# Stores of g on ScalarE's queue, and single-bank sums for the last products

## The chip, the cores and the metric

The kernel runs on one core of one Trainium2 chip. The metric is the device time of one execution in microseconds (us): here the median of three runs. Beside it stands one profiled execution, whose trace the text reads. A core has five engines with a queue of their own: TensorE (PE, matrix products into PSUM), VectorE (DVE), ScalarE (ACT), GpSimd (POOL) and SyncE (SP, which here only issues DMA transfers). Each works its queue off in order; semaphores tie them together.

## The reference

A retention layer (attention with a decaying state) and behind it a two-layer feed-forward block:

```python
for t in range(S):
    state = gamma[None, :, None, None] * state + np.einsum('bhd,bhe->bhde', k[:, :, t], v[:, :, t])
    y[:, :, t] = scale * np.einsum('bhd,bhde->bhe', q[:, :, t], state)
...
h = x @ w_in
relu6 = np.clip(h + 3.0, 0.0, 6.0)
g = h * relu6 / 6.0
return (g @ w_out).astype(np.float32)
```

q, k and v have shape (4, 8, 768, 64), so x has 3072 tokens of 512 values; w_in is 512 x 2048 and w_out 2048 x 512. The weights arrive as 64-bit floats.

## The kernel before

The tokens are cut into six tiles of 512 (`u` = 0 to 5, `UT` = 512), the 2048 inner columns into 16 blocks of 128 (`jj`).

**First phase, lines 473 to 499.** For every pair (`u`, `jj`) `mm1` (line 459) computes one tile of h: 12 products on TensorE into one PSUM bank (three buffers, `ps_h`), then a relu on ScalarE (line 468), then a multiplication with a bound of 6 on VectorE (line 469), which leaves g in SBUF (three buffers, `hpool`), then a store of g to memory (line 470), 256 KB, issued by SP. The 12 products are 4 blocks of the inner dimension times 3: each operand is split by `split` (line 139, ScalarE and VectorE at lines 140 and 141) into a rounded part and a rest, and three of the four products of parts are summed.

Between these tiles TensorE does the attention in bursts (`burst`, line 260, in the first half of the tokens, `chunk_burst`, line 355, in the second); a state in PSUM (`uz`) is copied out by ScalarE (lines 323 and 353) before TensorE adds the next piece. The rows of k, q and v that a burst needs are loaded by SP (`load`, line 218), and some of them are multiplied on GpSimd (lines 231, 235, 245).

In the same stretch the weights are built. `fetch` (line 109) has SP load a block of 64-bit words into a tile `st` (two buffers); `to_f32` (line 114) makes 32-bit floats of it with five operations on VectorE (lines 122 to 136) and one on ScalarE (line 126); then they are split. The first four blocks of w_in are fetched with the attention's first rows; the further ones by the loop over `steps`, line 486, the fifth between the first and the second tile of h. Blocks of w_out follow at the places that `WHEN` lists.

**Second phase, lines 502 to 615.** Tiles of g are read back from memory into `gv`, two blocks of a pair and two token tiles at a time, summed or subtracted (a scheme with seven products of blocks in the place of eight), split into `gc`, and multiplied with w2 (line 587): three super-blocks `sb`, in each four groups of sums (`GROUPS`), in each four steps `c`. The sums `acc` of groups 0 and 2 stand on the right side of PSUM, those of 1 and 3 on the left; a sum is one tile of two banks, one for each half `h` of its output rows. At the end of a group VectorE or ScalarE reads the sums (lines 534 and 537), and SP stores the output (line 541). The last group of the last super-block is read and stored in halves (`parts`).

**What sets the order.** TensorE's order is that of the program (`manual_schedule`). On the other engines the framework orders the instructions of a queue by its own estimate, with hints such as `high_priority` and `issue_after`; once ordered, the queue is fixed. It also finds the semaphores that an instruction must wait for, by tile. Of the two first-phase queues that the change touches, SP's holds all loads and all stores in one line.

Of the kernel before, what the change touches and what calls it, by code (L numbers as in the profile page):

```python
# [19 lines left out]
P = 128  # L20
# [8 lines left out]
def retention_ffn(ctx: ExitStack, tc: tile.TileContext, qkv, w_in, w_out, dvs, dqs, dkc, dqc, dmc, out, B, H, S, D):  # L29
# [429 lines left out]
    def mm1(u, jj):  # L459
        h = ps_h.tile([P, UT], F32, tag="h", name=nm("h"))  # L460
        for k in range(NK):
            t, o = w1_block(jj, k)
            for n, (a, b) in enumerate(((0, 0), (0, 1), (1, 0))):
                nc.tensor.matmul(  # L464
                    h, t[:, o, a], xs[u][b][:, k], start=k + n == 0, stop=(k, n) == (NK - 1, 2), skip_group_check=True
                )
        g = hpool.tile([P, UT], F32, tag="g", name=nm("g"))
        nc.scalar.activation(out=g, in_=h, func=AF.Relu, bias=three)  # L468
        ins = nc.vector.scalar_tensor_tensor(out=g, in0=g, scalar=6.0, in1=h, op0=ALU.min, op1=ALU.mult)  # L469
        nc.sync.dma_start(out=gd[jj // 2][:, jj % 2, u * UT : (u + 1) * UT], in_=g)  # L470
        return ins.ins

    order = ExitStack()
# [8 lines left out]
    for n, (u, jj) in enumerate(steps):  # L482
        if (u, jj) == (NU - 1, 0):
            att.close()
            late = ctx.enter_context(tc.tile_pool(name="late", bufs=1, side="right", reuse_waits="tile"))
        while n_w1 < min(NF, jj + 4):
            build_w1(n_w1)
            n_w1 += 1
        if jj in WHEN.get(u, ()):
            build_w2(n_w2)  # L490
            n_w2 += 1
        end = mm1(u, jj)
        if n < UR:
            advance(UR + 2 + n)
        elif u == 1:
            advance(2 * UR + 2 + int((jj + 1) / NF * UR + 0.5))
        elif 1 < u < NU - 1:
            advance(UR * (u + 1) + 2 + int((jj + 1) / NF * UR + 0.5))
    ph1.close()

# [3 lines left out]
        for n in ("gv0", "gv1", "gc2", "v", "p", "gc0", "gc1", "q")  # L504
    }
    ps_o = [
        ctx.enter_context(tc.tile_pool(name=f"ps_o{i}", bufs=1, space=PSUM, reuse_waits="tile", side=side))
        for i, side in enumerate(("right", "left"))
# [29 lines left out]

    def store(sb, t, m, src, h):
        o = out[m * HM : (m + 1) * HM, (2 * sb + t) * UT : (2 * sb + t + 1) * UT].rearrange("(h p) n -> p h n", p=P)  # L540
        nc.sync.dma_start(out=o[:, h], in_=src[:, h])

    for sb in range(NT // TB):
        for g, ids in enumerate(GROUPS):
            acc = {i: ps_o[g % 2].tile([P, 2, UT], F32, tag=f"o{n}", name=nm("o")) for n, i in enumerate(ids)}
            for c in range(NFP // CP):
# [35 lines left out]
                for i, gc in zip(ids, ops):  # L582
                    for h in range(2):
                        for jj in range(CP):
                            j = c * CP + jj
                            for n, (x, y) in enumerate(((0, 0), (0, 1), (1, 0))):
                                nc.tensor.matmul(  # L587
                                    acc[i][:, h],
                                    w2c[j][:, RIGHT[i], x, h],
# [4 lines left out]
                                )  # L594
            whole = slice(0, 2)
            if g == 0:
# [6 lines left out]
            elif g == 2:  # L603
                acc6(kept["u"], acc[7], kept["u"])
                dve_add(kept["p"], kept["u"], kept["p"])
                dve_add(kept["q"], kept["u"], kept["q"])
                store(sb, 1, 0, kept["p"], whole)
                store(sb, 1, 1, kept["q"], whole)
            else:
                parts = (whole,) if sb < NT // TB - 1 else (slice(0, 1), slice(1, 2))  # L610
                for k, i, m in (("s", 2, 0), ("v", 3, 1)):
                    for h in parts:
                        acc6(kept[k][:, h], acc[i][:, h], kept[k][:, h])
                        store(sb, 0, m, kept[k], h)
    order.close()
# [97 lines left out]
```

## Time and profile before

| what | value |
|---|---|
| three runs | 590.0, 590.01, 592.35 us |
| median | 590.01 us |
| the profiled execution | 590.15 us |
| its span, first to last instruction | 588.4 us |
| mean granted TensorE clock | 0.992 |
| moved to and from memory | 117.05 MB, mean 199 GB/s |
| transfers of g to memory | 96 of 256 KB, all issued by SP |

The span is the part of the profiled execution in which instructions run; 1.75 us lie around it. A line such as `L469 DVE` names the line of the kernel and the engine; where a row has a bracket, it is the idle time of that engine just before the instruction, and the instruction that ended it. `PEclk` or the clock column is the share of TensorE's full clock that was granted. A transfer has an issue (busy time in its issuer's queue) and a time to landing that comes after.

### The profile page before, as it was taken

How to read it: one execution, taken by the hardware profiler on the slowest of the kernel's cores; microseconds unless marked ns; L12 is line 12 of the kernel's file. 1: busy time of each engine (PE TensorE's matmuls, PEld its weight loads, DVE VectorE, ACT ScalarE, POOL GpSimd, SP SyncE). 2: the span in 40 equal slices, each digit the busy share in tenths (PEclk: the TensorE clock that was granted, in tenths of full speed). 3: DMA queues.
4: the chain of work that ended last, by engine and by line, in shares of the span. 5: the costliest groups of instructions: out<-in, count | busy, mean ns of one | idle time of the engine just before them, and what ended most of it. 6: DMA issues, size and time to landing. Idle time of an engine off the chain costs nothing.

```text
span 588.4 us, 11368 instructions
## 1 busy us (share of the span) xinstructions
PE 573.7 (98%) x4604; PEld 471.3 (80%) x4604; DVE 416.6 (71%) x588; ACT 249.1 (42%) x393; POOL 35.2 (6%) x39
## 2 busy tenths in 40 slices
PE   8888999999999999999999999999999999999996
PEld 7766788777888888888888888888888888888885
DVE  4879999999533498333225989769587698866871
ACT  5773445443423344332324555444335343344430
POOL 1001000101221121121000000000000000000000
PEclk9988999999999999999999999999999999999999
DMA  8966677665965467555243457564844747635611
GB/s 321 391 234 208 218 254 233 233 216 187 300 231 174 160 225 250 189 182 174 106 135 115 162 194 253 176 218 143 277 152 144 243 143 262 211 114 181 205 72 71
DMA packets 58884, 117.05 MB, mean 199 GB/s; under 512 B 5968, under 2 KB 6352, under 8 KB 58832
## 3 DMA queue, kind: packets, MB, share of 16 engines
q1 hardware_dynamic: 58688, 116.31, 58.7%
q8 instruction: 36, 0.59, 0.4%
q14 instruction: 16, 0.13, 0.1%
q10 hardware_dynamic: 144, 0.02, 0.0%
HBM read 84.85 MB, written 31.46 MB: 198 GB/s over the span
## 4 chain that ended last, share of the span: by engine, by line
PE 78%; DVE 14%; DMA 3%; issue 3%; ACT 1%; SPq 1%; DVEq 0%; ACTq 0%
PE o L587 39%; PE h L464 33%; DVE g L469 2%; DMA st<-in_w_in 2%; PE uz L349 2%; DVE w L141 2%; DVE wb L128 2%; PE sc L349 1%; DVE am L327 1%; DVE we L131 1%; DVE ww L134 1%; PE y L349 1%; DVE we L122 1%; DMA early<-in_qkv 1%; DVE wb L123 1%
## 5 line engine op out<-in xcount | busy, mean ns | idle before, releaser
L464 PE MATMUL h<-x,w 128*128 128x512 f32 x1152 | 271.1, 394 | 2.8 <-DVE x L141 1.2
L464 PEld LDWEIGHTS h<-x,w 128*128 128x128 f32 x1152 | 214.9, 189 | 51.4 <-DVE g L469 3.1
L587 PE MATMUL o<-gc,w 128*128 128x512 f32 x1008 | 231.5, 392 | 0.0
L587 PEld LDWEIGHTS o<-gc,w 128*128 128x128 f32 x1008 | 189.2, 188 | 42.1
L469 DVE SCALAR_TENSOR_TENSOR g<-g,h 128x512 f32<-128x512 f32 x96 | 65.3, 683 | 84.7 <-ACT g L468 84.7
L468 ACT ACTIVATE g<-h,three 128x512 f32<-128x512 f32 x96 | 65.2, 683 | 101.1 <-PE h L464 98.3
L140 ACT ACTIVATE gc<-gv 128x1024 fp32r<-128x1024 f32 x48 | 50.8, 1060 | 65.8 <-PE o L587 55.1
L141 DVE TENSOR_TENSOR gc<-gv,gc 128x1024 fp32r<-128x1024 f32 x48 | 58.6, 1221 | 22.8 <-ACT gc L140 22.7
L140 ACT ACTIVATE gc<-spare 128x1024 fp32r<-128x1024 f32 x36 | 38.2, 1061 | 48.9 <-PE o L587 37.5
L141 DVE TENSOR_TENSOR gc<-spare,gc 128x1024 fp32r<-128x1024 f32 x36 | 43.9, 1220 | 8.6 <-ACT gc L140 8.5
L140 ACT ACTIVATE w<-ww 128x384 fp32r<-128x384 f32 (+2 forms) x34 | 18.7, 555 | 49.0 <-DVE ww L134 46.6
L126 ACT ACTIVATE we<-we,ebias 128x512 int32<-128x512 int32 x32 | 22.9, 717 | 12.2 <-DVE we L122 12.2
L134 DVE SCALAR_TENSOR_TENSOR ww<-wb,we 128x512 f32<-128x512 f32 x32 | 24.5, 765 | 0.6
L235 POOL TENSOR_TENSOR qs<-qt,dq 128x512 f32<-128x512 f32 x12 | 16.7, 1388 | 95.9 <-PE y L349 59.9
L128 DVE SCALAR_TENSOR_TENSOR wb<-st,wb 128x512 f32<-128x512 uint32 x32 | 21.9, 685 | 0.2
L141 DVE TENSOR_TENSOR w<-ww,w 128x384 fp32r<-128x384 f32 (+2 forms) x34 | 19.9, 590 | 3.1 <-ACT w L140 3.1
L131 DVE SCALAR_TENSOR_TENSOR we<-st,we 128x512 int32<-128x512 int32 x32 | 21.9, 683 | 0.0
L96 DVE TENSOR_TENSOR spare<-gv 128x1024 f32<-128x1024 f32 x12 | 14.7, 1222 | 8.0 <-DMA gv<-gd 8.0
L122 DVE TENSOR_SCALAR we<-st 128x512 int32<-128x512 int32 x32 | 14.3, 446 | 8.3 <-DMA st<-in_w_in 8.1
L93 DVE TENSOR_TENSOR spare<-spare,gv 128x1024 f32<-128x1024 f32 x12 | 14.6, 1220 | 5.3 <-DMA gv<-gd 5.3
L93 DVE TENSOR_TENSOR gv<-gv 128x1024 f32<-128x1024 f32 x12 | 14.7, 1223 | 4.6 <-DMA gv<-gd 4.5
L241 ACT ACTIVATE early<-early,cst_sb 128x64 f32<-128x64 f32 x64 | 16.4, 335 | 3.6 <-DMA early<-in_qkv 3.6
(73 smaller groups left out, 395.8 us busy)
## 6 DMA issues: line engine op xcount, KB each, us to landing
gd<-g SPq DMA_DIRECT2D x96, 256.0 KB, 2.7
gv<-gd SPq DMA_DIRECT2D x48, 512.0 KB, 4.9
gv<-gd SPq DMA_DIRECT2D x48, 256.0 KB, 3.1
st<-in_w_in SPq DMA_DIRECT2D x16, 512.0 KB, 4.0
st<-in_w_out SPq DMA_DIRECT2D x16, 512.0 KB, 3.9
early<-in_qkv SPq DMA_DIRECT2D x28, 256.0 KB, 6.0
kt<-in_qkv SPq DMA_DIRECT2D x16, 256.0 KB, 3.8
qt<-in_qkv SPq DMA_DIRECT2D x16, 256.0 KB, 4.2
```

The costliest lines, as they stand in the source:

```text
L93: return nc.vector.tensor_tensor(out=out_, in0=a, in1=b, op=ALU.subtract)
L126: nc.scalar.activation(out=e, in_=e, func=AF.Relu, scale=8.0, bias=ebias)
L128: nc.vector.scalar_tensor_tensor(out=y, in0=lo.bitcast(U32), scalar=2.0**-32, in1=b, op0=ALU.mult, op1=ALU.add)
L131: nc.vector.scalar_tensor_tensor(out=e, in0=hi, scalar=-2147483648, in1=e, op0=ALU.bitwise_and, op1=ALU.bitwise_or)
L134: nc.vector.scalar_tensor_tensor(out=w, in0=y, scalar=2.0**-20, in1=e.bitcast(F32), op0=ALU.mult, op1=ALU.mult)
L140: nc.scalar.activation(out=hi, in_=src, func=AF.Copy)
L141: nc.vector.tensor_tensor(out=lo, in0=src, in1=hi, op=ALU.subtract)
L349: nc.tensor.matmul(out_, lhs, rhs, start=start, stop=True, skip_group_check=True)
L464: nc.tensor.matmul(h, t[:, o, a], xs[u][b][:, k], start=k + n == 0, stop=(k, n) == (NK - 1, 2), skip_group_check=True)
L468: nc.scalar.activation(out=g, in_=h, func=AF.Relu, bias=three)
L469: ins = nc.vector.scalar_tensor_tensor(out=g, in0=g, scalar=6.0, in1=h, op0=ALU.min, op1=ALU.mult)
L587: nc.tensor.matmul(acc[i][:, h], w2c[j][:, RIGHT[i], x, h], gc[:, y, jj], start=j == 0 and n == 0, stop=j == NFP - 1 and n == 2, skip_grou ...
```

## The change

Two parts. First, the store of a tile of g is no longer issued by SP at its place in the program. It is put on a list, and issued by ScalarE behind the relu of the next tile (`to_memory(relu.ins)`); the last one is issued behind the last multiplication (`to_memory(end)`). Second, in the last group of the last super-block each half of a sum is a PSUM tile of its own, of one bank; to make room for them the two pools of sums are closed first. The four halves are read and stored one by one, and the last half is read and stored in two pieces of 256 columns (`BLK`), the second piece stored by ScalarE.

```diff
--- before.py
+++ after.py
@@ -465,10 +465,20 @@
                     h, t[:, o, a], xs[u][b][:, k], start=k + n == 0, stop=(k, n) == (NK - 1, 2), skip_group_check=True
                 )
         g = hpool.tile([P, UT], F32, tag="g", name=nm("g"))
-        nc.scalar.activation(out=g, in_=h, func=AF.Relu, bias=three)
+        relu = nc.scalar.activation(out=g, in_=h, func=AF.Relu, bias=three)
         ins = nc.vector.scalar_tensor_tensor(out=g, in0=g, scalar=6.0, in1=h, op0=ALU.min, op1=ALU.mult)
-        nc.sync.dma_start(out=gd[jj // 2][:, jj % 2, u * UT : (u + 1) * UT], in_=g)
+        to_memory(relu.ins)
+        waiting.append((gd[jj // 2][:, jj % 2, u * UT : (u + 1) * UT], g))
         return ins.ins
+
+    waiting = []
+
+    def to_memory(after):
+
+        for out_, g in waiting[:1]:
+            with tc.issue_after(after):
+                nc.scalar.dma_start(out=out_, in_=g)
+        del waiting[:1]
 
     order = ExitStack()
     order.enter_context(tc.manual_schedule(engines={mybir.EngineType.PE}))
@@ -496,6 +506,7 @@
             advance(2 * UR + 2 + int((jj + 1) / NF * UR + 0.5))
         elif 1 < u < NU - 1:
             advance(UR * (u + 1) + 2 + int((jj + 1) / NF * UR + 0.5))
+    to_memory(end)
     ph1.close()
 
 
@@ -503,8 +514,9 @@
         n: ctx.enter_context(tc.tile_pool(name=f"left_{n}", bufs=1, reuse_waits="tile"))
         for n in ("gv0", "gv1", "gc2", "v", "p", "gc0", "gc1", "q")
     }
+    ends = ctx.enter_context(ExitStack())
     ps_o = [
-        ctx.enter_context(tc.tile_pool(name=f"ps_o{i}", bufs=1, space=PSUM, reuse_waits="tile", side=side))
+        ends.enter_context(tc.tile_pool(name=f"ps_o{i}", bufs=1, space=PSUM, reuse_waits="tile", side=side))
         for i, side in enumerate(("right", "left"))
     ]
     CP = 2
@@ -536,13 +548,19 @@
     def acc6(out_, ps, other):
         nc.vector.scalar_tensor_tensor(out=out_, in0=ps, scalar=SIXTH, in1=other, op0=ALU.mult, op1=ALU.add)
 
-    def store(sb, t, m, src, h):
+    def store(sb, t, m, src, h=slice(0, 2), to=slice(0, UT), eng=nc.sync):
         o = out[m * HM : (m + 1) * HM, (2 * sb + t) * UT : (2 * sb + t + 1) * UT].rearrange("(h p) n -> p h n", p=P)
-        nc.sync.dma_start(out=o[:, h], in_=src[:, h])
+        eng.dma_start(out=o[:, h, to], in_=src[:, h, to])
 
     for sb in range(NT // TB):
         for g, ids in enumerate(GROUPS):
-            acc = {i: ps_o[g % 2].tile([P, 2, UT], F32, tag=f"o{n}", name=nm("o")) for n, i in enumerate(ids)}
+            last = sb == NT // TB - 1 and g == len(GROUPS) - 1
+            if last:
+                ends.close()
+                ps_e = ctx.enter_context(tc.tile_pool(name="ps_e", bufs=1, space=PSUM, reuse_waits="tile", side="left"))
+            acc = {i: ps_o[g % 2].tile([P, 2, UT], F32, tag=f"o{n}", name=nm("o")) for n, i in enumerate(ids)} if not last else {
+                i: [ps_e.tile([P, UT], F32, tag=f"e{i}{h}", name=nm("o")) for h in range(2)] for i in ids
+            }
             for c in range(NFP // CP):
                 with ExitStack() as first:
                     if sb == 0 and g == 0 and c == 0:
@@ -585,14 +603,13 @@
                             j = c * CP + jj
                             for n, (x, y) in enumerate(((0, 0), (0, 1), (1, 0))):
                                 nc.tensor.matmul(
-                                    acc[i][:, h],
+                                    acc[i][h] if last else acc[i][:, h],
                                     w2c[j][:, RIGHT[i], x, h],
                                     gc[:, y, jj],
                                     start=j == 0 and n == 0,
                                     stop=j == NFP - 1 and n == 2,
                                     skip_group_check=True,
                                 )
-            whole = slice(0, 2)
             if g == 0:
                 scaled(kept["p"], acc[4], -SIXTH)
                 scaled(kept["q"], acc[5])
@@ -604,14 +621,19 @@
                 acc6(kept["u"], acc[7], kept["u"])
                 dve_add(kept["p"], kept["u"], kept["p"])
                 dve_add(kept["q"], kept["u"], kept["q"])
-                store(sb, 1, 0, kept["p"], whole)
-                store(sb, 1, 1, kept["q"], whole)
+                store(sb, 1, 0, kept["p"])
+                store(sb, 1, 1, kept["q"])
             else:
-                parts = (whole,) if sb < NT // TB - 1 else (slice(0, 1), slice(1, 2))
                 for k, i, m in (("s", 2, 0), ("v", 3, 1)):
-                    for h in parts:
-                        acc6(kept[k][:, h], acc[i][:, h], kept[k][:, h])
-                        store(sb, 0, m, kept[k], h)
+                    if not last:
+                        acc6(kept[k], acc[i], kept[k])
+                        store(sb, 0, m, kept[k])
+                    else:
+                        for h in range(2):
+                            for n in range(2 if (i, h) == (3, 1) else 1):
+                                to = slice(n * BLK, (n + 1) * BLK) if (i, h) == (3, 1) else slice(0, UT)
+                                acc6(kept[k][:, h, to], acc[i][h][:, to], kept[k][:, h, to])
+                                store(sb, 0, m, kept[k], h, to, nc.scalar if n else nc.sync)
     order.close()
```

## The prediction

> **What bounds the kernel now.** I read the busy times of the page first, then the busy times by stage, then the chain of work that ended last, and only then the queue that the change empties.
>
> ```profile
> PE 573.7 (98%) x4604; PEld 471.3 (80%) x4604; DVE 416.6 (71%) x588; ACT 249.1 (42%) x393; POOL 35.2 (6%) x39
> ```
>
> TensorE is busy 98% of the 588.4 us. A share over the whole span hides who leads in a stage, so here are three stages of 30 us (columns: stage, length, then busy time and count of PE, PEld, DVE, ACT, POOL, then granted clock, DMA share, GB/s).
>
> ```profile
> 30.00:60.00 30.00, 26.61 (x298) 21.23 (x299) 25.65 (x42) 15.79 (x44) 2.09 (x2) 0.89 0.64 214
> 60.00:90.00 30.00, 29.83 (x239) 24.21 (x239) 29.49 (x53) 14.92 (x27) 1.05 (x1) 1.00 0.72 236
> 90.00:120.00 30.00, 30.00 (x200) 24.45 (x198) 29.76 (x56) 14.26 (x25) 2.19 (x2) 1.00 0.69 228
> ```
>
> From 60 to 120 us VectorE is as full as TensorE: whatever delays VectorE there delays the end, and a head start that both have at 60 us is kept. From 30 to 60 us neither is full: 4.35 us of VectorE and 3.39 us of TensorE are idle, and the clock is below 1. Time can only be won there and at the very end, as the chain shows (start, length, what).
>
> ```profile
> 37.49 4.61 DMA st<-in_w_in
> ...
> 352.61 231.33 PE o L587 x1008
> 583.96 0.69 DVE kept_v L537
> ```
>
> The second phase is one unbroken row of 1008 products, 231.33/1008 = 0.2295 us each; no transfer of g lies on it, and after the last product come a VectorE operation and a store. In front stands a transfer of w_in. Its cause is in SP's queue. First the wait of SP at line 470 (total us, times, longest), then SP's issues in order of time:
>
> ```profile
> SPq L470 <- DVE g L469: 134.7, 75, 5.1
> ```
> ```profile
> 29.55 0.33 SPq L218 DMA_DIRECT2D kn<-in_qkv  x1
> 37.11 0.33 SPq L470 DMA_DIRECT2D gd<-g  x1
> 37.49 1.10 SPq L111 DMA_DIRECT2D st<-in_w_in  x2
> ...
> 39.58 0.45 SPq L218 DMA_DIRECT2D vn<-in_qkv  x1
> ```
>
> SP sits 7 us before the first store of g, and two fetches of w_in and the loads of k, q, v stand behind it. VectorE shows what that costs (the bracket is idle time before, and who ended it):
>
> ```profile
> 27.26 0.68 DVE L128 SCALAR_TENSOR_TENSOR wb<-st,wb 128x512 f32<-128x512 uint32 x1
> ...
> 32.91 0.69 DVE L131 SCALAR_TENSOR_TENSOR we<-st,we 128x512 int32<-128x512 int32 x1
> ...
> 36.40 0.69 DVE L469 SCALAR_TENSOR_TENSOR g<-g,h 128x512 f32<-128x512 f32 x1 [2.07 <-ACT g L468]
> ...
> 42.12 0.43 DVE L122 TENSOR_SCALAR we<-st 128x512 int32<-128x512 int32 x1 [0.79 <-DMA st<-in_w_in]
> ...
> 45.57 1.25 DVE L122 TENSOR_SCALAR we<-st 128x512 int32<-128x512 int32 x1
> ```
>
> The `st` buffers were free at 27.94 and about 33.6 us (ends of lines 128 and 131 of the third and fourth weight block), yet the fetch went out at 37.49, and VectorE waited 0.79 us for it.
>
> **The change part by part.** *The fetch.* Without line 470 on SP the fifth fetch follows `kn`, at 29.9 us, and the sixth goes out at about 33.7. With the 4.61 us to landing of the chain's row the data is there at 34.5, before VectorE asks for it at 41.3. So the wait of 0.79 us goes. What is late next? If VectorE keeps its order, it goes on with work until this operation, 1.25 us where the same one takes 0.43 above: 0.82 us longer, beside a GpSimd operation that waited for `vn`.
>
> ```profile
> 45.49 1.05 POOL L245 TENSOR_TENSOR vn<-vn,cst_sb 128x512 f32<-128x512 f32 x1 [42.27 <-DMA vn<-in_qkv]
> ```
>
> That load moves about 4 us up with the queue, so GpSimd will meet another operation of VectorE, or one of its idle moments. Bounds 0 and 0.82 us gained; I take half, 0.4. Together 1.2 us, with 0 and 1.6 as the ends when the order stays. Behind it stands TensorE's one long wait here, which has room for it:
>
> ```profile
> 49.20 0.90 PE L281 MATMUL sc<-early 64*64 64x128 f32 x32 [2.24 <-DVE am L327]
> ```
>
> After that stage the clock row reads (stage, length, PE, clock, DMA share, GB/s):
>
> ```profile
> 50.01:53.43 3.42, 3.42 (x40) 0.50 0.70 196
> ```
>
> The half clock costs TensorE 1.71 us of work. [...] I do not add it: VectorE sets the pace behind this place, and it is idle for no long stretch that TensorE could fill.
>
> *The stores on ScalarE.* 96 issues go to ScalarE. The nearest rows are its one issue of before and the 96 on SP (ns: shortest, median, longest), and their time to landing:
>
> ```profile
> 0.80 0.40 ACTq L68 DMA_DIRECT2D cst_sb<-in_decays_v  x1
> ```
> ```profile
> L470 SPq DMA_DIRECT2D gd<-g x96: 319/326/892, 37.1 to 354.1; - x96
> ...
> DMA to landing us min/median/max: 2.0/2.7/5.7
> ```
>
> 96 times 0.33 to 0.40 is 31 to 38 us of ScalarE's queue, against 339 us in which it isn't busy. Each issue also waits for line 469 of the tile before. Normally that is long done when the next relu ends. The worst place is where two relus run close:
>
> ```profile
> 129.34 1.25 ACT L468 ACTIVATE g<-h,three 128x512 f32<-128x512 f32 x2
> 134.77 0.52 ACT L140 ACTIVATE w<-ww 128x384 fp32r<-128x384 f32 x1 [4.19 <-DVE ww L134]
> ```
> ```profile
> 131.16 0.68 DVE L469 SCALAR_TENSOR_TENSOR g<-g,h 128x512 f32<-128x512 f32 x1
> ```
>
> The store behind the second relu (over at 130.6) waits until 131.84; queued behind it is a copy that starts at 134.77 anyway. Nothing lost. Where ScalarE has something urgent next is an attention burst: the copy of the state must be read before TensorE writes `uz` again.
>
> ```profile
> 169.16 0.69 ACT L468 ACTIVATE g<-h,three 128x512 f32<-128x512 f32 x1 [2.03 <-PE h L464]
> 169.84 0.38 ACT L353 ACTIVATE state<-uz 128x256 f32<-128x256 f32 x1
> ```
> ```profile
> 170.50 0.24 PE L349 MATMUL uz<-vn,kn 64*64 64x64 f32 x2
> ```
>
> The copy ends at 170.22, 0.28 us ahead. An issue that runs beside the relu costs 0; one that holds ScalarE after it costs 0.40 - 0.28 = 0.12 us in each of 11 bursts, 1.3 us; the longest issue, 0.89, costs 0.61 each, 6.7 us. I take 0, since 0.33 to 0.40 fits beside a relu of 0.69 that is already under way. The buffers of g (three) come back later: the store starts one tile after its product instead of at once. At 12 products of 0.2295, a tile is 2.75 us; relu n+3 starts 4.8 us after relu n+1 ends, an issue of 0.4 and a landing of 2.7 end 3.1 after it. Only landings over 4.4 us would hold a relu, and the three banks of `h` give TensorE two more tiles. In before such a wait came once:
>
> ```profile
> ACT g L468 <- DMA gd<-g: 2.7, 1, 2.7
> ```
>
> I count nothing for it either way; its 2.7 us is the bound of a gain or a loss, and it was hidden by those banks.
>
> *The last store*, queued at the end of the phase, waits for line 469 of the last tile:
>
> ```profile
> 353.23 1.05 ACT L140 ACTIVATE gc<-gv 128x1024 fp32r<-128x1024 f32 x1
> 353.36 0.69 DVE L469 SCALAR_TENSOR_TENSOR g<-g,h 128x512 f32<-128x512 f32 x1 [1.79 <-ACT g L468]
> ...
> 355.11 1.22 DVE L141 TENSOR_TENSOR gc<-gv,gc 128x1024 fp32r<-128x1024 f32 x1
> ```
>
> If the copy at 353.23 has to wait behind it, it starts at 354.05 + 0.40, 1.2 us late; the subtraction behind it then ends at about 356.8. TensorE wants the pair after the 24 products of the first step, 352.61 + 5.5 = 358.1. Covered by 1.3 us; uncovered it would cost up to 1.2.
>
> *The last products.* Sums of one bank each free VectorE from waiting for the other half, and the last half is cut in two (the third view gives shortest, median and longest landing; the fourth a 256-column VectorE operation).
>
> ```profile
> 581.24 1.29 DVE L537 SCALAR_TENSOR_TENSOR spare<-o,spare 128x512 f32<-128x512 f32 x2 [8.68 <-PE o L587]
> 581.95 0.94 SPq L541 DMA_DIRECT2D out<-spare  x2
> 583.96 1.29 DVE L537 SCALAR_TENSOR_TENSOR kept_v<-o,kept_v 128x512 f32<-128x512 f32 x2 [1.43 <-PE o L587]
> 584.67 0.93 SPq L541 DMA_DIRECT2D out<-kept_v  x2
> ```
> ```profile
> DMA to landing us min/median/max: 2.0/2.5/3.2
> ```
> ```profile
> L141 DVE TENSOR_TENSOR w<-ww,w 128x256 fp32r<-128x256 f32 x4 | 1.5, 418 | 0.0
> ```
>
> Both halves of `kept_v` start after the last product, and the second ends at 583.96 + 1.29 = 585.25. Now the first half is done before the last product, and two pieces of 0.42, overlapping by the 0.08 that back-to-back operations show (two of 0.69 in 1.29), end at 584.72: 0.53 us earlier. The last transfer is half as large and goes out on a queue of its own: 0 to 0.3 us more. I take 0.6, ends 0.2 and 0.9. The new banks lie where the sums of the second group stood, long read; should they wait for the third group's reader instead, one VectorE operation on 1024 columns, 1.22 us as at 355.11, would stand in front of the last group. I take 0.
>
> **Sum.** 590.15 us (the profiled execution; its span 588.4) - 1.2 - 0.6 = 588.35. The median of the runs is 590.01, 0.14 lower: **588.2 us**.
>
> **The rivals.** *Further ahead.* With the fetch early, VectorE may be given the fifth block's first operations in the 2.07 us that it idles before 36.40. Then 2.07 + 0.79 + 0.82 + 0.6 = 4.3 us: 585.7. For it: those operations need only the landed block and its scratch buffers. Against: VectorE runs in the order in which it was queued, and nothing in the trace shows that this order moves.
>
> *Only the end moves.* SP's time to issue was on no path, and VectorE, full from 60 us, eats the head start or GpSimd's stall moves to as bad a place. Then 590.01 - 0.6 = 589.4. [...] The trace speaks against it at one place, the 0.79 us wait. If even the halves of a sum still wait for each other, the change doesn't do what it says, and 0.2 us is left: 589.8.
>
> *Slower.* The issue holds ScalarE behind the relu, and the state copies are late in 11 bursts. It decides from 0.28 us on, and eats the gain of 1.8 from 0.28 + 1.8/11 = 0.44 us. At 0.8 us, near the longest issue of SP, it costs 5.7: 590.01 - 1.8 + 5.7 = 593.9. For it: ScalarE is one queue. Against: the medians, 0.33 and 0.40.
>
> **How the numbers follow.** The forecast 0.48 (its own range 587.0 to 589.2), further ahead 0.22, only the end 0.18, slower 0.12. The range 585.4 to 590.9 takes in the first three and the small costs named above (1.3 for the bursts, 1.2 for the banks), and leaves out the last. About 0.5%, 2.95 us, is what a measurement of this kernel can tell from no change. Faster by more: further ahead and a little of the forecast, 0.26. Slower by more: most of the last rival, 0.10. Within: 0.64.
>
> **What would show it.** SP issues `st` near 30 us and VectorE's wait of 0.79 before line 122 is gone; TensorE's wait at 49.2 is shorter than 2.24; the second phase starts about 1.2 us before 352.6 and still takes 231.3; VectorE ends about 0.8 us behind the last product instead of 1.3. Wrong would be: a new wait of ScalarE for line 469 or for the stores of g with TensorE waiting behind it, `uz` products that wait for the state copy, or a first stage in which VectorE's order is another.

## The result, and the profile after

The changed kernel took **588.35 us**, median of 6 runs (587.09 to 588.67). Six runs of the kernel before beside it had a median of 592.32 (590.0 to 593.43): ratio 0.9936, 95% interval 0.9912 to 0.9961. On another chip it was 587.89 against 591.12, ratio 0.9947 (0.9927 to 0.9966). So it is faster by about half a per cent, 3 to 4 us; the forecast time of 588.2 was met, though the forecast gain was 1.8. Where the gain lies, and why it is larger than the sum, takes the rest of this text.

Profiled, it took 588.39 us with a span of 586.7, 1.76 less than the profile before. Busy times and the issue row of g from its page:

```profile
PE 571.7 (97%) x4604; PEld 469.8 (80%) x4604; DVE 416.2 (71%) x589; ACT 249.4 (43%) x393; POOL 36.5 (6%) x39
...
gd<-g ACTq DMA_DIRECT2D x96, 256.0 KB, 2.6
```

All 96 stores come from ScalarE now, at 2.6 us to landing. Its chain of waits (start, length, what):

```profile
77.38 3.08 DMA st<-in_w_in
...
351.85 231.33 PE o L605 x1008
583.19 0.42 DVE kept_v L549
```

The second phase starts 0.76 us earlier than at 352.61 and lasts the same 231.33. The fetch of w_in near 37 us is off the chain. SP's queue after, which answers to the rows with `kn`, `gd<-g`, `st`, `vn` of before:

```profile
29.90 0.33 SPq L218 DMA_DIRECT2D kn<-in_qkv  x1
30.62 3.49 SPq L111 DMA_DIRECT2D st<-in_w_in  x2
34.20 0.38 SPq L218 DMA_DIRECT2D kt<-in_qkv  x1
...
35.11 0.42 SPq L218 DMA_DIRECT2D vn<-in_qkv  x1
35.57 0.43 SPq L218 DMA_DIRECT2D kn<-in_qkv  x1
36.05 0.43 SPq L218 DMA_DIRECT2D vn<-in_qkv  x1
```

Nothing of g stands in front of the two fetches: they go out from 30.62 on instead of 37.49. Note the last row: the load of `vn` for the next row, at 46.44 in the kernel before, is 10 us earlier too. VectorE and TensorE after (the bracket is idle time before, and who ended it):

```profile
41.18 0.82 DVE L141 TENSOR_TENSOR x<-xr,x 128x512 fp32r<-128x512 f32 x1 [0.84 <-ACT x L140]
41.92 0.42 DVE L122 TENSOR_SCALAR we<-st 128x512 int32<-128x512 int32 x1
```
```profile
48.77 0.90 PE L281 MATMUL sc<-early 64*64 64x128 f32 x32 [1.63 <-DVE am L327]
```

The wait of 0.79 for `st` in front of line 122 is gone, and TensorE's wait has shrunk from 2.24 to 1.63. At the end, VectorE's last rows:

```profile
581.84 0.69 DVE L549 SCALAR_TENSOR_TENSOR kept_v<-o,kept_v 128x512 f32<-128x512 f32 x1 [0.67 <-PE o L605]
583.19 0.76 DVE L549 SCALAR_TENSOR_TENSOR kept_v<-o,kept_v 128x256 f32<-128x256 f32 x2 [0.67 <-PE o L605]
```

The half sums no longer wait for each other, and the last one ends at 583.95.

### The profile page after: what moved, and what is told of

Same layout as the page of the kernel before. It is cut to its first block, busy times and chain, and to the rows that moved or that the text cites. A ratio compares the mean times of both kernels' runs of the same rounds, so it can differ in the third digit from the quotient of the medians.

```text
span 586.7 us, 11328 instructions
## 1 busy us (share of the span) xinstructions
PE 571.7 (97%) x4604; PEld 469.8 (80%) x4604; DVE 416.2 (71%) x589; ACT 249.4 (43%) x393; POOL 36.5 (6%) x39
## 4 chain that ended last, share of the span: by engine, by line
PE 78%; DVE 14%; DMA 3%; issue 3%; ACT 1%; SPq 1%; ACTq 0%; DVEq 0%
PE o L605 39%; PE h L464 33%; DVE g L469 2%; DVE we L131 2%; PE uz L349 2%; DMA st<-in_w_in 2%; DVE wb L128 2%; DVE am L327 2%; PE sc L349 1%; DVE ww L134 1%; PE y L349 1%; DVE w L141 1%; DVE x L141 1%; DMA early<-in_qkv 1%; DVE xr L301 1%
```

## The experiments

Each was timed beside runs of the kernel before on its chip. To see where time is won I read from each trace when the first product of every h tile starts, and compare the distance between two such starts with that in the profile before. The columns are: where, between 30 and 60 us, a stage of half clock starts; from the first to the seventh tile (the early time); "GpSimd", how much longer than their usual (median) time those VectorE operations took that ran beside a GpSimd operation, summed from 30 us to the seventh tile; won or lost (-) at the start of the 22nd tile (near 111 us), the 35th (157) and the 59th (237); from the first tile to the second phase; and from the start of the last product to the end. All in us.

| profile | half clock at | 1st to 7th | GpSimd | 22nd | 35th | 59th | to 2nd phase | tail |
|---|---|---|---|---|---|---|---|---|
| before | 32.95, 50.01 | 35.11 | 1.35 | | | | 322.27 | 4.87 |
| changed | 32.30 | 33.42 | 0.40 | -1.00 | -0.85 | 0.47 | 321.36 | 3.91 |
| changed, again | 32.80, 49.86 | 34.43 | 1.08 | -1.02 | -1.18 | 0.46 | 322.83 | 3.90 |
| stores alone | none | 32.67 | 1.23 | -1.01 | -1.11 | 0.28 | 321.09 | 4.87 |
| end alone | none | 33.07 | 1.06 | -0.45 | 0.00 | -0.93 | 321.67 | 3.93 |
| first store alone | none | 31.95 | 0.49 | 0.01 | -0.04 | -0.70 | 320.02 | 5.07 |
| first store and end | 48.06 | 33.07 | 1.67 | 0.02 | 0.00 | -1.53 | 322.01 | 4.12 |
| changed, no decays | none | 31.49 | 0.00 | 0.02 | -0.85 | 0.47 | 317.76 | 3.92 |
| first and late stores | 32.56 | 34.04 | 1.03 | -0.03 | -0.04 | 0.47 | 320.77 | 3.91 |
| decays on ScalarE | none | 31.43 | 0.00 | 0.02 | -1.45 | 0.47 | 318.22 | 3.92 |
| both of these | 32.43 | 32.88 | 0.00 | -0.13 | -0.02 | 0.47 | 319.90 | 3.92 |
| at once | none | 32.03 | 1.19 | -0.12 | -0.19 | -0.19 | 320.10 | 3.91 |

Half clock and the GpSimd column differ between executions of one kernel (see changed, and changed again), so one early time can't simply be set against another. With the GpSimd column taken off, the early times fall into order. The end alone, with its first store on SP, has 32.01. Stores alone, first store alone, first store and end, no decays, and decays on ScalarE have 31.40 to 31.49. Changed, first and late stores, and both of these, which have a stage near 32 us, have 32.88 to 33.02, and changed, again, 33.35. Three things can be read from that. The first store on SP costs 0.5 to 0.6 (0.4 between before, 33.76, and changed, again). A stage near 32 us costs 1.4 to 1.6. A stage near 50 us costs nothing in first store and end, and 0.3 to 0.5 in changed, again. (At once has 30.84; there VectorE waits 0.27 in place of 0.83 us for an x copy of ScalarE.)

**The stores alone.** The diff's part with `to_memory` and `waiting`, the last products as before.

```diff
-        nc.sync.dma_start(out=gd[jj // 2][:, jj % 2, u * UT : (u + 1) * UT], in_=g)
+        to_memory(relu.ins)
+        waiting.append((gd[jj // 2][:, jj % 2, u * UT : (u + 1) * UT], g))
```

> The kernel before with the stores of g alone moved to ScalarE, each behind the next tile's relu; the last products as before. Theory F (forecast: the first store's place holds up two weight fetches, VectorE sets the pace, 1.2 us come back): start of the second phase 1.2 us earlier than 352.44, time 1.2 us under the kernel before. Theory C (clock: the larger part of what the early stage gives is that TensorE's idle stretch at 49 us becomes too short to be followed by 3.41 us at half clock; the stores that land late take some of it back): only one half-clock stage between 30 and 60 us, a lead of 1.5 to 2.0 us at the fourth and fifth h tile, and 0.5 to 1.0 us left at the start of the second phase, as in the changed kernel. Both: the end behind the last product as before (VectorE some 1.3 us behind).

589.51 us (12 runs) against 590.94 (35): ratio 0.9973 (0.9955 to 0.999). The profile had no half-clock stage, where one was expected, so the lead at the fifth tile was 2.69 and not 1.5 to 2.0; 0.97 were left at the second phase. As theory C has it, some is lost again later: 1.0 at the 22nd tile and 1.1 at the 35th, of which only the second will turn out to come from late stores.

**The end alone.**

```diff
-            acc = {i: ps_o[g % 2].tile([P, 2, UT], F32, tag=f"o{n}", name=nm("o")) for n, i in enumerate(ids)}
+            last = sb == NT // TB - 1 and g == len(GROUPS) - 1
...
+            acc = {i: ps_o[g % 2].tile([P, 2, UT], F32, tag=f"o{n}", name=nm("o")) for n, i in enumerate(ids)} if not last else {
+                i: [ps_e.tile([P, UT], F32, tag=f"e{i}{h}", name=nm("o")) for h in range(2)] for i in ids
+            }
```

> The kernel before with the last products alone changed (a tile per bank, the last bank in two halves); stores of g stay on SP. Theory F: 0.6 us (0.2 to 0.9) off the end, first phase unchanged. Rival from the two traces: 0.97 us, the difference there from the start of the last product to the end (4.87 against 3.91). Both: two half-clock stages between 30 and 60 us as before, start of the second phase within 0.3 us of 352.44.

589.58 us (12 runs), ratio 0.9977 (0.9954 to 0.9999). The tail fell from 4.87 to 3.93, 0.95 us, at the rival's 0.97 rather than at 0.6. "Both" missed: no half-clock stage, though the first phase is that of the kernel before. This gives a comparison with no such stage: 33.07 from the first to the seventh tile, against 32.67 with all stores moved. VectorE's wait for `st` is 0.60 us in this profile.

**The first store alone.**

```diff
+        to_memory(relu.ins)
+        if (u, jj) == (0, 0):
+            waiting.append((gd[0][:, 0, 0:UT], g))
+        else:
+            nc.sync.dma_start(out=gd[jj // 2][:, jj % 2, u * UT : (u + 1) * UT], in_=g)
```

> The kernel before with one store moved: that of the very first tile of g goes to ScalarE, behind the second tile's relu; the other 95 stay on SP. Theory F: the whole early gain of 1.2 us, since only this store stands ahead of weight fetches that VectorE waits for. Theory C: the same fetches go out near 30 us; the second half-clock stage goes away if TensorE's gap at 49 us falls from 2.24 to about 1.6 us, and then the lead at the fifth tile is 1.5 to 2.0 us, and as no store of tiles 21 and 34 lands late behind ScalarE, 1.2 to 2.0 us are left at the start of the second phase: more than with all stores moved. A third theory (all stores matter): below 0.4 us.

589.68 us (12 runs), ratio 0.9973 (0.9952 to 0.9995), the same as with all 96. At no half-clock stage it takes 31.95 to the seventh tile, 1.12 less than 33.07 and near the forecast's 1.2, where all 96 bring 0.40. Do the other 95 lose 0.72? GpSimd and VectorE with the stores alone, then GpSimd with the first store alone:

```profile
41.85 1.04 POOL L245 TENSOR_TENSOR vn<-vn,cst_sb 128x512 f32<-128x512 f32 x1 [38.63 <-DMA vn<-in_qkv]
43.08 1.26 POOL L245 TENSOR_TENSOR vn<-vn,cst_sb 128x512 f32<-128x512 f32 x1 [0.19 <-DMA vn<-in_qkv]
```
```profile
42.25 1.19 DVE L131 SCALAR_TENSOR_TENSOR we<-st,we 128x512 int32<-128x512 int32 x1
43.47 1.42 DVE L134 SCALAR_TENSOR_TENSOR ww<-wb,we 128x512 f32<-128x512 f32 x1
44.92 0.43 DVE L122 TENSOR_SCALAR we<-st 128x512 int32<-128x512 int32 x1
```
```profile
40.90 1.58 POOL L245 TENSOR_TENSOR vn<-vn,cst_sb 128x512 f32<-128x512 f32 x1 [37.69 <-DMA vn<-in_qkv]
48.13 1.46 POOL L245 TENSOR_TENSOR vn<-vn,cst_sb 128x512 f32<-128x512 f32 x1 [5.65 <-DMA vn<-in_qkv]
```

With all stores gone from SP, nothing holds the second `vn` load, and two decays on GpSimd follow each other at 41.85 and 43.08. Two VectorE operations that take 0.69 elsewhere then take 1.19 and 1.42. With the second store still on SP the second decay comes at 48.13, and the two meetings cost 0.49 in place of 1.23: that is the 0.72. So the store that held up a wanted fetch also held up a GpSimd operation, but that this is what made it cheaper isn't shown. In first store and end the decays lie as far apart (40.57 and 49.47) and cost 1.67; in the changed kernel's first profile they come close together (40.41 and 43.01) and cost 0.40. Which operation of VectorE a decay meets decides, and it varies as much between two profiles of one kernel (0.40 and 1.08). What the first store's place costs for sure is the wait for `st`, **0.4 to 0.6 us**.

**Filler products.** Sixteen filler products more were asked for (the count of row 6).

```diff
-    BUSY = {0: 11, 2: 3, 3: 5, 4: 5}
+    BUSY = {0: 11, 2: 3, 3: 5, 4: 5, 6: 16}
```

> The kernel before with 16 filler products (128 columns, written to a bank that nobody reads, about 0.12 us each, 1.9 us together) ahead of the third h tile, where TensorE sits idle for 2.24 us; nothing else moves, SP's order is that of before. Theory F (VectorE sets the pace behind 49 us, a faster TensorE would only wait): 0 to 0.3 us faster. Theory C (the half clock that follows the idle stretch costs by itself): no half-clock stage near 50 to 53 us and 1.3 to 1.7 us faster at the start of the second phase. A rival: the fillers run past the idle stretch and cost up to 1 us.

593.17 us (12 runs) against 590.94, ratio 1.0034 (1.0013 to 1.0055): 2.2 us lost, more than the rival had. The fillers on TensorE, then VectorE and TensorE behind them:

```profile
44.06 3.84 PE L412 MATMUL idle<-mask 128*128 128x128 f32 x32
52.88 3.03 PE L464 MATMUL h<-x,w 128*128 128x512 f32 x12
```
```profile
51.21 1.42 DVE L134 SCALAR_TENSOR_TENSOR ww<-wb,we 128x512 f32<-128x512 f32 x1
...
56.81 0.68 DVE L301 TENSOR_TENSOR xr<-y,early 128x512 f32<-128x512 f32 x1
```
```profile
57.55 0.67 PE L268 MATMUL y<-early,state 64*64 64x128 f32 x16 [1.64 <-DVE xr L301]
```

Each filler shows as two products, and they stood ahead of the third tile, while the idle stretch lies behind it. TensorE made up for them at once: the fourth tile starts at 52.88, against 52.79 in the profile before, since the idle stretch and the second half-clock stage are gone. The loss comes behind that, and from VectorE. The edit also changed the order of its queue: in the profile before, `xr` follows line 134 at 52.95, while here seven operations on weights and one on g stand between the two, and TensorE waits 1.64 us for it. So "nothing else moves" failed, and the price of a stage can't be read from this run.

**The changed kernel again.**

> The changed kernel again, beside the next three. If the two parts measured alone add up (0.9973 and 0.9977 of the kernel before), the ratio is 0.995; if the earlier 0.9936 holds, 1.5 us more come from the two together.

587.89 us (7 runs) against 591.12 (18): 0.9947 (0.9927 to 0.9966). The two parts add up (0.9973 times 0.9977 is 0.995). Its profile, 589.68 us, was its slowest run, and had the same two half-clock stages as the profile before, so these two can be laid side by side: 0.68 won up to the seventh tile (0.27 of it in the GpSimd column), 1.02 lost at the 22nd, 0.6 won between, 1.18 lost at the 35th, 0.46 won at the 59th, 0.14 lost behind it, 0.97 won in the tail. With the first tile 0.03 earlier that is the 0.44 us between the spans (588.40 and 587.96).

The loss at the 35th tile, by ScalarE's rows and TensorE's:

```profile
152.19 0.33 ACTq L480 DMA_DIRECT2D gd<-g  x1
153.53 0.69 ACT L468 ACTIVATE g<-h,three 128x512 f32<-128x512 f32 x1 [1.73 <-DMA gd<-g]
153.61 0.33 ACTq L480 DMA_DIRECT2D gd<-g  x1
157.16 0.69 ACT L468 ACTIVATE g<-h,three 128x512 f32<-128x512 f32 x1 [2.94 <-DMA gd<-g]
...
157.74 0.38 ACT L353 ACTIVATE state<-uz 128x256 f32<-128x256 f32 x1
```
```profile
158.22 0.27 PE L349 MATMUL uz<-vn,am 64*64 64x64 f32 x2 [0.98 <-issue]
```

Read it upwards. The `uz` product comes 0.98 us late, right after the copy of the state; the copy stands on ScalarE behind a relu; the relu waited 2.94 us for a buffer of g whose store had not landed (up to 4.9 us from issue to landing here). The banks of h hide this late relu from the h products (from 150 to 160 us the 0.98 is TensorE's only wait), but not the copy queued behind it.

**The first store and the end.** Both edits above in one kernel.

> The kernel before with only the very first store of g on ScalarE (behind the second relu), the other 95 on SP, and the last products as changed. Theory P (only the first store pays; 95 stores on ScalarE cost something, by the second GpSimd operation moved beside VectorE near 43 us, by VectorE's order near 106 us and by stores that land late near 153 us): first phase 2.0 to 2.3 us ahead of the profile before where both run at full clock, and the end 0.95: some 587 us, 0.5 to 1.5 us faster than the changed kernel. Rival (the stores on ScalarE pay throughout, by freeing SP's queue, as near 236 us): the changed kernel is faster by 0.5 us or more.

588.49 us (12 runs), ratio 0.9955 (0.9941 to 0.997): not faster than the changed kernel. Theory P is right up to the 58th tile (no loss at the 22nd and 35th), and then 1.53 us go at once. ScalarE and TensorE there:

```profile
235.38 0.69 ACT L468 ACTIVATE g<-h,three 128x512 f32<-128x512 f32 x1 [4.27 <-DMA gd<-g]
235.97 0.38 ACT L353 ACTIVATE state<-uz 128x256 f32<-128x256 f32 x1
```
```profile
236.44 0.27 PE L349 MATMUL uz<-vn,am 64*64 64x64 f32 x2 [1.79 <-POOL qs L235]
```

And SP's queue ahead of it:

```profile
226.17 0.37 SPq L233 DMA_DIRECT2D dq<-in_decays_q  x1
226.59 0.46 SPq L218 DMA_DIRECT2D kt<-in_qkv  x1
227.10 0.42 SPq L218 DMA_DIRECT2D qt<-in_qkv  x1
227.62 0.38 SPq L218 DMA_DIRECT2D vn<-in_qkv  x1
228.09 0.38 SPq L111 DMA_DIRECT2D st<-in_w_out  x1
229.28 2.90 SPq L474 DMA_DIRECT2D gd<-g  x3
```

The same chain as at the 35th tile, with the roles changed: five fetches go out ahead of three stores of g, which then take 4.7 to 6.0 us to land, the relu waits 4.27 us for one of them, and copy and `uz` product follow late. (The profile names GpSimd as the releaser of that product, but its `qs` had run at 234.36; the copy ended at 236.35.) The waits of TensorE for `uz` between 100 and 350 us, in the profile before, with the end alone, the first store alone, and both:

```profile
PE uz L349 <- issue: 0.3, 1, 0.3
```
```profile
PE uz L349 <- POOL qs L235: 1.2, 1, 1.2
```
```profile
PE uz L349 <- POOL qs L235: 1.0, 1, 1.0
```
```profile
PE uz L349 <- POOL qs L235: 1.8, 1, 1.8
```

**The profile before had the smallest of these.** What the stores on ScalarE win here is 0.5 us against that profile, but 1.2 to 2.0 us against the three others. (The kernel with fillers, whose stores are on SP as well, loses 1.10 at this place.)

**Four buffers of g.** There was no room for a fourth, so the sums of a w_out block share a buffer with its exponent words.

```diff
-    hpool = ph1.enter_context(tc.tile_pool(name="hpool", bufs=3))
+    hpool = ph1.enter_context(tc.tile_pool(name="hpool", bufs=4))
...
-        sm = wst.tile([P, 4, P], F32, tag="ws", name=nm("ws"))
+        sm = wst.tile([P, 4, P], F32, tag="we", name=nm("ws"))
```

> The changed kernel with four buffers of g in place of three; to make room, the sums that the w_out blocks build share one buffer with the exponent words (both 2 KB a partition). Theory L (relus that wait for a late landing of the store three tiles back cost the 0.8 to 1.1 us lost at the 35th tile): relus no longer wait 9.6 us for stores, no loss of lead at that tile, 0.8 us faster than the changed kernel, less what the shared buffer costs VectorE between 100 and 240 us (0 to 0.5 us). Rival (the loss there is contention of transfers and the uz product's own issue): no gain.

601.42 us (4 runs), ratio 1.0166 (1.0137 to 1.0194). The relus wait for no store to land any more. Beside those that wait for their h products, two waits are left, for which the profile names VectorE's sums (total us and times):

```profile
  DVE ws L93: 5.2, 2
```

One of the two is at the 35th tile, where 1.94 us are lost although theory L had none. The relu comes 2.50 us late there, at 154.27; in front of it on ScalarE stands a store's issue, at 153.84, which had to wait for a late g (line 469, over at 153.81). So a late buffer is not the only way in which these stores can hold a relu. The shared buffer seems to cost far more than the 0.5 allowed for it: the last w_out block is finished only in the second phase, where TensorE waits 2.61 and 1.62 us for its input and then takes 6.40 us for 16 products that need 3.67 at the second phase's 0.2295 each. So the experiment doesn't tell what a fourth buffer by itself would bring; that stays open.

```profile
359.70 0.69 DVE L141 TENSOR_TENSOR w<-ws,w 128x512 fp32r<-128x512 f32 x1
```
```profile
363.81 0.49 PE L605 MATMUL o<-gc,w 128*128 128x512 f32 x1 [2.61 <-ACT gc L140]
```

**Without the decays on GpSimd.**

```diff
-        elif r >= AHEAD:
-            decay(r)
```

> The changed kernel without GpSimd's four multiplications of vn by the decays (rows 8 to 11): that part of the computation is left out. Theory G (a GpSimd operation slows the VectorE operation beside it by 0.15 to 0.8 us): every VectorE operation there takes its usual 0.42 or 0.69 us, 0.4 to 1.2 us come back up to the seventh tile and up to 0.9 us near 106 us. Rival (those long VectorE operations wait for something else, their input or the clock): the long operations stay, below 0.2 us. If VectorE's pace does not matter there, the time stays though the operations are short.

585.27 us (6 runs), ratio 0.9902 (0.9879 to 0.9925), 2.6 us under the changed kernel. Up to the seventh tile it takes 31.49 against 32.67 with all stores moved, both without a half-clock stage: **1.18 us**, where the GpSimd column falls from 1.23 to 0. The loss at the 22nd tile is gone too (0.02 won instead of 1.0 lost); that at the 35th, laid to late stores, stays at 0.85. Theory G holds in both places.

**Stores on ScalarE for the first tile and from the 41st on.**

```diff
+        if len(tiles) == 1 or len(tiles) > 40:
+            waiting.append((out_, g))
+        else:
+            nc.sync.dma_start(out=out_, in_=g)
```

> The changed kernel, with the stores of g on ScalarE only for the first tile and from the 41st tile on; those of tiles 2 to 40 go back to SP. Theory P (stores on ScalarE lose 1.2 us near 43 us by two GpSimd operations close together, 1.0 us near 106 us by VectorE's order, 0.9 to 1.2 us near 153 us by late landings, and win 0.5 to 2.0 us near 236 us where SP queues six fetches ahead of three stores): keeps the win and drops the losses, so lead of 2.0 to 2.2 us up to the 57th tile at one half-clock stage as in the kernel with first store and end only, no loss of lead at the 59th; time 586.0 to 587.0 where the kernel before has 591.1 and the changed one 587.9. Rival (the lead gained early is given back later, whatever brings it): 587.5 to 588.5, no faster than the changed kernel.

587.19 us (12 runs) against 590.69 (24): 0.9932 (0.9911 to 0.9952). No loss at the 22nd and 35th tiles, 0.47 won at the 59th: the three middle terms behave as theory P says. The early lead did not: 34.04 to the seventh tile, where 33.07 had been seen with one half-clock stage too. But that stage lay near 48 us, where it costs nothing, and this one near 32. So the lead was 0.9 and not 2.0, and the time misses its 586.0 to 587.0 by a little. From the changed kernel (0.9947) it can't be told apart.

**The decays on ScalarE.** In the changed kernel rows 8 to 11 are treated like rows 0 to 7.

```diff
-        if r < AHEAD:
+        if r < CHUNKED:
             for h in range(H):
                 nc.scalar.activation(
```

> The changed kernel with the four multiplications of vn by the decays (rows 8 to 11) done by ScalarE, 8 short operations of about 0.34 us a row as in rows 0 to 7, in place of one GpSimd operation. Theory G (GpSimd's operations slow VectorE beside them; without them at all the kernel took 585.3): 2.6 us less than the changed kernel, minus what 2.7 us a row of ScalarE's time cost: 585.5 to 587. Rival (ScalarE's eight operations stand ahead of relus and x copies that VectorE waits for): as slow as the changed kernel or slower by up to 2 us.

**585.15 us** (7 runs) against 590.69: 0.9912 (0.9877 to 0.9947), the fastest version that computes everything; six of its seven runs (584.3 to 587.38 in all) lie under every run of the changed kernel (587.09 to 589.68). The ratio's interval still touches that of the changed kernel (0.9927 to 0.9966). ScalarE's 8 operations lose 0.96 between the 7th and the 21st tile (a relu stands behind them at 77.48, and VectorE waits 0.94 us for it), which is won back by the 30th.

**At once.** Every store in the program's order, not behind the next relu.

```diff
-        to_memory(relu.ins)
-        waiting.append((gd[jj // 2][:, jj % 2, u * UT : (u + 1) * UT], g))
+        nc.scalar.dma_start(out=gd[jj // 2][:, jj % 2, u * UT : (u + 1) * UT], in_=g)
```

> The changed kernel with every store queued on ScalarE at once, in the program's order, and not behind the next tile's relu. If the place behind the next relu matters: ScalarE stands still from each relu until VectorE has made g (0.7 us and more where VectorE is full), relus and state copies come later, and the first phase is longer by 2 us or more. If it does not: within 0.5 us of the changed kernel (587.9).

588.53 us (12 runs), ratio 0.9963 (0.9938 to 0.9988). The standstill is there, but it costs little: waits of ScalarE that the changed kernel doesn't have (total us, times, longest).

```profile
ACT g L468 <- DVE g L469: 15.7, 11, 2.3
```

At 0.64 us over the changed kernel and with intervals that overlap, it is neither 2 us nor surely nothing. That the place behind the next relu matters is not shown. Its one profile even loses less at the 22nd tile (0.12) and at the 35th (0.19) than any with all stores behind the next relu and the decays on GpSimd.

**Late stores and decays together.**

> Both edits together: stores of g on ScalarE only for the first tile and from the 41st on, and the decays of rows 8 to 11 on ScalarE. If their gains are separate (0.9932 alone, 0.9912 alone, the changed kernel 0.9947), the ratio to the kernel before is 0.990 (585.0 where that one has 591). If each mends the same loss (VectorE's late g products), it stays at 0.991 to 0.992. With ScalarE's operations on the path of the relus it is worse than the decays alone.

587.01 us (6 runs) against 591.19 (10): 0.9921 (0.9893 to 0.9949). By the median the gains don't add, though the interval takes in the 0.990 of separate gains. Runs at a granted clock of 0.999 or more took 585.1 in this kernel and 584.3 to 586.3 with the decays alone, so the two are alike.

## Why the prediction came out as it did

**The bound and the places.** Right: the early stage and the end could be won, the second phase kept its 231.33 us, and SP's store of the first g held two fetches that VectorE waited for. That time can be won nowhere else was wrong: the 59th tile, near 237 us, was a place too. "Only the end moves" is out: the stores alone give 0.9973, with an interval that ends at 0.999. Two places in these traces show that SP's queue cost more than the time to issue (0.33 us a store): the first store of g waited for its data and held two fetches behind it, SP for 7 us near 30 (before), and near 230 (first store and end) three stores of g stand behind five fetches and take 4.7 to 6.0 us to land.

**The fetch, 1.2 us.** The wait of 0.79 went, as forecast. In the end alone it was 0.60, and without it the early time falls by 0.4 to 0.6 once the GpSimd column is taken off. The step that failed is "Bounds 0 and 0.82 us gained; I take half, 0.4", for the GpSimd operation that moves up with its load. The profile before has two such meetings, the 0.82 at 45.57 and another of 0.53 at 51.81, together 1.35. I counted one, and the change moves both. What they cost afterwards differs from one execution to the next: 0.40 and 1.08 in the changed kernel, 1.23 with the stores alone. So the term was a gain of 0.95 in the changed kernel's first profile and of 0.27 in its second; against the end alone (1.06) the stores alone have a loss of 0.17. The lower bound should have reached below nothing, and the real prize, 1.2 us for having no decays on GpSimd at all, was in no term.

**The clock.** "I do not add it: VectorE sets the pace" was right for the stage near 50 us that it was said of. In first store and end such a stage starts at 48.06 (stage, length, busy PE, PEld, DVE, ACT, POOL, clock, DMA share, GB/s):

```profile
48.06:51.47 3.41, 3.41 (x40) 3.16 (x35) 3.41 (x5) 0.38 (x1) 1.04 (x1) 0.50 0.62 180
```

VectorE is full in it, and the early time less the GpSimd column is 31.40, as without a stage. The two profiles of the changed kernel differ by such a stage and by 1.01 us (34.43 and 33.42), but 0.68 of that is the GpSimd column. The stage near 32 us, which the profile before has as well, is in no term, and it is the one that costs, 1.4 to 1.6 of 1.71 at most. Whether it comes isn't settled by the change (below).

**The stores, 0 us.** The issue itself cost nothing in the row at 153.61, as forecast: it starts 0.08 us after its relu, and its 0.33 us run beside the relu's 0.69. "Hidden by those banks" failed: landings of up to 4.9 us hold a relu, and the state copy behind that relu holds `uz`, 0.85 to 1.18 us in one burst. That was the slower rival's chain (late state copies), with another first link and in one burst instead of 11; a wait of ScalarE for the stores of g with TensorE waiting behind it was among the signs that the prediction named for being wrong. The 1.0 us at the 22nd tile, which goes when the decays leave GpSimd, was in no term. On the other side the forecast had nothing for the 59th tile, where stores on SP cost 0.5 to 2.0 us; the wait of 2.7 us that I quoted and called hidden was its first link.

**The last products, 0.6 us.** The mechanism was right and the size low: 0.95 by themselves, 0.97 in the changed kernel. VectorE ends 0.54 us earlier behind the same product, as worked out (0.53). The other 0.43 us is the way from VectorE's end to the end of the span: 588.40 - 585.25 = 3.15 before, 586.67 - 583.95 = 2.72 after. I had allowed 0 to 0.3 for it and taken almost nothing.

**The last store and the banks, 0.** Right: the second phase lasts as long in all profiles but that with four buffers.

**The sum.** The forecast 588.2 hit the time because terms that it lacked nearly cancel, and its base was the kernel before on a good day: 590.0, where 87 later runs have a median of 590.97 (586.8 to 595.7). That the number was met is luck. (Its own range, 587.0 to 589.2, isn't the one that the ends of its terms give: 590.01 less 0.2 to 2.5 is 587.5 to 589.8.) Against the profile before, with the same two half-clock stages, the change wins 0.44 us; at the 59th tile a typical profile before would give 0.7 to 1.5 more, so 1.1 to 1.9. The measured 3.1 and more isn't all explained by that. Some of the rest is clock: its mean over 87 runs of the kernel before was 0.9951, over 13 of the changed one 0.9962, which is 0.65 us of granted time and at most that much of run time. Between half a microsecond and 2 us stay open; the draw of the GpSimd column is wide enough for that (0.40 to 1.67 in the profiles that have the decays on GpSimd), but no run shows that it is the reason.

## What to carry to other kernels

A transfer that waits for its data at the head of an in-order queue is a gate (SP stood 7 us before the first store of g here, with two fetches behind it): when it is moved, ask for every issue behind it what it releases. Work that gets in the way of a full engine is better taken away than moved: the decays on GpSimd cost 0.4 to 1.7 us wherever they fell, and giving them to ScalarE brought the early time to its lowest. A late buffer is hidden only if everything queued behind its waiter on the same engine is hidden as well (here the state copy was not, and 0.85 to 1.18 us went in one burst). One profile before is one draw: here its luckiest place (0.3 us where others had 1.0 to 1.8) was worth as much as the effect sought. And before two early times are compared, what differs by chance is to be listed and taken off, the place of a half-clock stage as well as their number.

## What the runs showed of the hardware

**Half clock differs between executions of one kernel.** The six runs of the changed kernel show mean granted clocks of 0.994 to 1.0. The clock's rows (stage, length, busy PE, PEld, DVE, ACT, POOL, then granted clock, DMA share, GB/s) in the profile after, and at the same time in the second profile of the same kernel:

```profile
50.00:53.42 3.42, 3.42 (x40) 2.94 (x37) 3.42 (x6) 1.42 (x3) 0.00 (x0) 1.00 0.51 189
```
```profile
49.86:53.27 3.41, 3.41 (x38) 3.20 (x35) 3.41 (x6) 1.15 (x3) 0.00 (x0) 0.50 0.47 150
```

Stages of half clock start at 32.95 and 50.01 in the profile before and at 32.80 and 49.86 in the second of the changed kernel: 17.06 us apart both times, five times 3.41. The length of TensorE's idle stretch ahead of line 281 doesn't by itself decide whether half clock follows near 50 us: it did after 2.24 us before and 2.08 in the second profile of the changed kernel; it didn't after 1.63 us in the first, 2.4 with the end alone and 2.48 with the stores alone. Nor is it the idle time in the 3.41 us ahead of a stage. That was 2.24 us ahead of 50.01 and 1.60 ahead of 32.95 in the profile before, and 1.59 ahead of 32.30 in the profile after; from 45.95 to 49.37 (which ends five times 3.41 us behind 32.30) the profile after has 1.63, and no half clock follows. So what starts a stage is not shown. A stage near 32 us makes the early times differ by 1.4 to 1.6 us, one near 50 by 0 to 0.5.

**GpSimd and VectorE operations that took longer side by side.** From the second profile of the changed kernel, GpSimd and then VectorE:

```profile
42.04 1.04 POOL L245 TENSOR_TENSOR vn<-vn,cst_sb 128x512 f32<-128x512 f32 x1 [38.81 <-DMA vn<-in_qkv]
43.26 1.27 POOL L245 TENSOR_TENSOR vn<-vn,cst_sb 128x512 f32<-128x512 f32 x1 [0.18 <-DMA vn<-in_qkv]
```
```profile
42.12 1.52 DVE L128 SCALAR_TENSOR_TENSOR wb<-st,wb 128x512 f32<-128x512 uint32 x1
43.55 0.68 DVE L469 SCALAR_TENSOR_TENSOR g<-g,h 128x512 f32<-128x512 f32 x1
44.15 0.93 DVE L131 SCALAR_TENSOR_TENSOR we<-st,we 128x512 int32<-128x512 int32 x1
```

The operations at 42.12 and 44.15 took 1.52 and 0.93, where their lines usually take 0.69. They end at 43.64 and 45.08, each 0.55 us after GpSimd's end (43.08 and 44.53), as if they had waited for most of it and then run. GpSimd's second operation, begun while VectorE's first was under way, took 1.27 in place of 1.04. The VectorE operation at 43.55, whose second input is in PSUM, took its usual 0.68; in the profiles before and after 29 operations of its line lay beside a GpSimd operation, and all took 0.67 to 0.69. That a GpSimd operation beside a full VectorE can have a price could have been forecast from the profile before (0.82 us at 45.57, 0.53 at 51.81); which operation it meets could not.
